# State attention and a hard-swish feed-forward network on one core: the first batch's tokens in two halves with even and odd tokens side by side, half steps for four tiles, and last output tiles scaled whole

## The chip, the core and the metric

The kernel runs on one core of a Trainium2 chip. The core has TensorE (PE) for matmuls, VectorE (DVE), ScalarE (ACT) and GpSimd (POOL), and SyncE (SP), whose queue issues most transfers. The metric is the device time of one execution in microseconds, the median of the runs shown.

## The reference

The input `x` has 8 batches of 8 heads, 512 tokens and 64 columns, and `state` has 32 state tokens for each batch and head. Tokens attend to states, and states to tokens; both results go through one network.

```python
scores = scale * x @ state.T ; a  = softmax(scores) ; xread = a @ state       # 512 tokens of a head
scores2 = scale * state @ x.T; a2 = softmax(scores2); sread = a2 @ x          # 32 states of a head
x = concatenate([xread, sread], tokens)   # as rows of 512 columns (8 heads x 64): 8 x 544 rows
h = x @ w_in                              # w_in 512 x 2048
g = h * clip(h + 3, 0, 6) / 6
out = g @ w_out                           # w_out 2048 x 512, out 4352 x 512 in float32
```

The weights lie in DRAM as 64-bit floats, and the kernel makes 32-bit values of them.

## The kernel before

**Steps.** The network is done in 144 steps of 128 of its 2048 inner columns: 16 steps for the 512 tokens of each batch, and 16 for the state reads of all batches together (b = 8). A step has a first product into a PSUM bank `ps_h` (`first`), ScalarE and VectorE make `g` of it, and a second product adds into four banks `acc` (`second`). Since `a @ state @ w_in` is the same as `a @ (state @ w_in)`, the kernel makes W' = state x W_in for each batch and chunk of four steps (`wprime`, L441) and multiplies the attention weights by it, so that the token reads themselves are never made. Nearly all products are sums of three products of rounded high and low parts (`product`, L733). The first four steps of batch 0 are plain float32 (L762 and L800). Steps run in segments: batch 0's first four, batch 1's first four, the rest of batch 0, more of batch 1, then the batches one by one, and the states' steps last.

**Weights.** `weight` loads a tile of W_in or W_out (L303), and turns 64-bit into 32-bit words: ScalarE takes low digits and scales (L308, L312), VectorE clamps, joins and sets the sign (L316, L320, L327). The first tiles are unpacked while the first batch's attention runs.

**Batch 0.** Its x is loaded into a staging tile by two transfers of four heads each, and VectorE copies it into `xb` (L414). A partition p holds the four neighbouring tokens 4p to 4p+3. TensorE turns the state (L489) and x (L510, into banks that ScalarE copies to `xT`, L515), makes scores by rows of tokens in two halves (L565), each of which needs all four parts of `xT`, and VectorE and ScalarE do a softmax along the 32 states (L527 maximum, L529 subtraction, L531 exponential, L533 sum, L537 multiplication). The result is turned back (L582) and copied to `a` (L587). The first step's product needs `a` of all 512 tokens. The states' own attention uses the scores by columns (`scores_by_columns`: four heads' 32 states as 32-column groups, 512 tokens wide, L441 in `all_heads`), exponentials, eight transposes (L663) and a read (L678). Batch 1 takes its scores by columns as well.

**Order.** The class `Plan` collects each instruction group with an engine (`T` TensorE, `V` VectorE, `S_` ScalarE, `Q` a transfer of SP), a cost and a rank, and a list scheduler sets the order of each engine from them when the program is built. Where it leaves TensorE nothing to do before the first step, fillers are put in (transposes of the identity into `ps_h`, L1026). Their number is fixed in the program.

**End.** The 256 rows of state reads are two output tiles of 128 x 512. Each is scaled by 1/6 in two column halves, one on ScalarE and one on VectorE (L824), and each half is stored by a transfer of its own (L857 on SP's queue, L854 on ScalarE's).

## Time and profile before

| | |
|---|---|
| median of 3 runs | 676.68 us (676.36 to 677.1) |
| profiled execution | 676.72 us, of which the span is 674.7 us |
| TensorE busy | 666.1 us (99%) |
| VectorE, ScalarE busy | 412.8 us (61%), 317.8 us (47%) |
| packets of transfers | 94429, 41.53 MB |

The span is the part between the first and the last event that the profiler shows; some 2.0 us lie outside it. Times in the trace count from the span's start. Busy shares are means over the whole span; the start, with its short dependent pieces of work, is another matter than the long row of matmuls behind it.

### The profile page before, as it was taken

To read this page: it belongs to the slowest core of one execution; us is meant where nothing else is said; L and a number is where in the kernel's file an instruction comes from. 1 tells how busy PE (TensorE), PEld (TensorE's weight loads), DVE (VectorE), ACT (ScalarE), POOL (GpSimd) and SP (SyncE) were. 2 spreads that over 40 slices of the span, in tenths; PEclk is the share of its full clock that TensorE was granted. 3 is DMA by queue.
4 is the path that set the end of the run, shared out by engine and by line. 5 is a ranking of instruction groups with operands and counts; after the bars stand their busy time and mean duration, and the time that the engine had idled before them with its cause. 6 is when DMAs were issued, how large, how long until landed. Compare 5 with 4: busy or idle time off the path is not lost.

```text
span 674.7 us, 9940 instructions
## 1 busy us (share of the span) xinstructions
PE 666.1 (99%) x4039; PEld 508.6 (75%) x4039; DVE 412.8 (61%) x702; ACT 317.8 (47%) x537; POOL 1.0 (0%) x7
## 2 busy tenths in 40 slices
...
GB/s 260 306 4 149 120 204 82 74 69 125 1 140 53 1 63 78 52 1 63 0 129 1 63 1 103 27 44 21 44 20 1 1 1 63 1 1 0 63 1 31
DMA packets 94429, 41.53 MB, mean 62 GB/s; under 512 B 82480, under 2 KB 85040, under 8 KB 94256
## 3 DMA queue, kind: packets, MB, share of 16 engines
...
q10 hardware_dynamic: 144, 0.13, 0.1%
q14 instruction: 14, 0.11, 0.1%
...
## 4 chain that ended last, share of the span: by engine, by line
PE 96%; DVE 1%; DMA 1%; ACT 1%; issue 0%; SPq 0%
PE acc L733 55%; PE ps_h L733 29%; PE ps_s L441 6%; PE acc L800 2%; PE ps_s L678 1%; PE ps_h L762 1%; PE ps_s L663 1%; DMA st_raw<-in_state_dram 1%; PE acc L510 0%; DVE early L320 0%; DVE s L533 0%; DVE tmp L537 0%; PE acc L582 0%; PE ps_s L693 0%; ACT tmp L531 0%
## 5 line engine op out<-in xcount | busy, mean ns | idle before, releaser
L733 PE MATMUL acc<-w_out_hi,g_hi 128*128 128x512 f32 x528 | 212.1, 402 | 0.0
L733 PE MATMUL acc<-w_out_hi,g_lo 128*128 128x512 f32 x528 | 206.2, 391 | 0.0
L733 PE MATMUL acc<-w_out_lo,g_hi 128*128 128x512 f32 x528 | 205.7, 390 | 0.0
L781 ACT ACTIVATE g<-ps_h,three 128x512 f32<-128x512 f32 (+1 forms) x144 | 95.6, 664 | 214.2 <-PE ps_h L733 212.5
L783 DVE SCALAR_TENSOR_TENSOR g<-g,ps_h 128x512 f32<-128x512 f32 (+1 forms) x144 | 94.1, 654 | 161.2 <-ACT g L781 161.2
L733 PEld LDWEIGHTS acc<-w_out_hi,g_hi 128*128 128x128 f32 x528 | 99.3, 188 | 47.6 <-ACT g L781 21.0
L246 ACT CAST g_hi<-g 128x512 fp32r<-128x512 f32 (+1 forms) x140 | 83.4, 597 | 86.0 <-DVE g L783 86.0
L247 DVE TENSOR_TENSOR g_lo<-g,g_hi 128x512 fp32r<-128x512 f32 (+1 forms) x140 | 91.6, 655 | 47.7 <-ACT g_hi L246 46.6
L733 PE MATMUL ps_h<-aT_hi,wp_hi 128*128 128x512 f32 (+1 forms) x312 | 116.3, 373 | 0.0
L733 PEld LDWEIGHTS acc<-w_out_hi,g_lo 128*128 128x128 f32 x528 | 99.1, 188 | 21.7
L733 PE MATMUL ps_h<-aT_hi,wp_lo 128*128 128x512 f32 (+1 forms) x312 | 114.6, 367 | 0.0
L733 PE MATMUL ps_h<-aT_lo,wp_hi 128*128 128x512 f32 (+1 forms) x312 | 114.6, 367 | 0.0
L733 PEld LDWEIGHTS acc<-w_out_lo,g_hi 128*128 128x128 f32 x528 | 99.3, 188 | 18.5
L733 PEld LDWEIGHTS ps_h<-aT_hi,wp_hi 128*128 128x128 f32 x312 | 58.8, 188 | 13.0 <-issue 2.2
L733 PEld LDWEIGHTS ps_h<-aT_lo,wp_hi 128*128 128x128 f32 x312 | 58.8, 188 | 10.8 <-issue 0.5
L733 PEld LDWEIGHTS ps_h<-aT_hi,wp_lo 128*128 128x128 f32 x312 | 58.8, 188 | 9.8
L247 DVE TENSOR_TENSOR wp_lo<-ps_s,wp_hi 128x512 fp32r<-128x512 f32 (+1 forms) x68 | 42.0, 637 | 3.8 <-ACT wp_hi L246 3.8
L246 ACT CAST wp_hi<-ps_s 128x512 fp32r<-128x512 f32 (+1 forms) x68 | 36.2, 549 | 7.5 <-PE ps_s L441 7.4
L441 PE MATMUL ps_s<-w_in,stT 64*32 64x512 f32 (+1 forms) x592 | 37.3, 561 | 0.0
L441 PEld LDWEIGHTS ps_s<-w_in,stT 64*32 64x32 f32 x592 | 6.7, 104 | 14.3 <-issue 10.9
L308 ACT ACTIVATE early<-early,eighth 128x1024 uint32<-128x1024 uint32 (+1 forms) x14 | 16.1, 1150 | 2.3 <-DMA early<-in_moe_w_in_dram 2.3
L531 ACT ACTIVATE tmp<-tmp 128x512 f32<-128x512 f32 x16 | 10.1, 631 | 14.5 <-DVE tmp L529 14.4
(103 smaller groups left out, 434.3 us busy)
## 6 DMA issues: line engine op xcount, KB each, us to landing
...
raw<-in_moe_w_out_dram SPq DMA_DIRECT2D x7, 512.0 KB, 7.7
ot<-in_x_dram SPq DMA_DIRECT2D x2, 512.0 KB, 3.4
early<-in_moe_w_in_dram SPq DMA_DIRECT2D x2, 512.0 KB
```

The lines of the kernel that those rows point to most:

```text
L246: S_(cost, rank, lambda: nc.scalar.copy(hi(), src()), reads, [writes[0]])
L247: V(cost, rank, lambda: nc.vector.tensor_tensor(lo(), src(), hi().bitcast(F32), op=ALU.subtract), [*reads, writes[0]], [writes[1]])
L308: nc.scalar.activation(low, low, AF.Identity, scale=0.92 * 2.0**-29, bias=eighth)
L441: nc.tensor.matmul(out[u][cols, :], made["stT", b][rows, cols], moving(q)[rows], start=True, stop=True,)
L531: S_(0.62, rank(2), lambda: nc.scalar.activation(bt(), bt(), AF.Exp, scale=SCALE), [], [bt_key])
L663: nc.tensor.transpose(bank(pe[g])[:, js], tmp(e_key[g])[:, js], ident)
L678: nc.tensor.matmul(bank(pr)[cols, u * D : (u + 1) * D], tmp(t_key[u])[:, j * P + q * NS : j * P + (q + 1) * NS], x_tile(b)[:, NG * q + u, ...
L733: nc.tensor.matmul(ps, l, r, start=start and k == 0, stop=stop and k == n - 1)
L762: nc.tensor.matmul(bank(ps), made["wp_32", (b, k)][:, g, fs], a_first(g), start=g == 0, stop=g == NG - 1)
L781: S_(cost + 0.05, n, lambda: nc.scalar.activation(g(), bank(ps)[:, :width], AF.Relu, bias=three), [ps], [g_key])
L783: V(cost, n, lambda: nc.vector.scalar_tensor_tensor(g(), g(), 6.0, bank(ps)[:, :width], op0=ALU.min, op1=ALU.mult), [ps], [g_key])
L800: nc.tensor.matmul(bank(acc), made["g_hi", n][:, js], plain_out[i][1](), start=opens, stop=closes)
```

## The change

The change has these parts.

- **x of batches 0 and 1 in another order.** A partition holds tokens of two halves k of 256 tokens, and of each half an even and an odd token i side by side, so that one transpose turns one head's 2 x 64 columns. Batch 0's x comes by two transfers, one for each half, straight into `xb`, without the staging tile and the copies. Batch 1's comes by one transfer. VectorE makes half of batch 0's copies to `xT`.
- **The state turned twice.** Since even and odd tokens now lie on the two halves of the partitions, the state is needed on both: four matmuls with the identity in place of one transpose.
- **Scores by halves.** The scores by rows of one half need only `xT` of that half. Scores by columns of batches 0 and 1 are 32 matmuls of 128 columns in place of 8 of 512, and the states' softmax takes its maxima and sums over two banks.
- **Half steps.** Each of the first four steps is done as two half steps of 256 tokens: two first products of 256 columns, a gate for each, and two second products for each. W' of these steps comes in four parts and is kept beside `a`, in the place of the third chunk of W_in.
- **Other ranks.** The ranks of the early loads, unpackings, scores and of the states' attention are other numbers, tiles 2 and 3 of W_in are loaded one by one, and what makes high and low parts of the first four W_out tiles is set earlier.
- **The end.** The two last tiles are scaled whole, the first by VectorE, the second by ScalarE, and stored by one transfer each, the first on SP's queue, the second on ScalarE's.

```diff
+        if b >= TURNED:
             for j in range(J):
                 def load(j=j):
-                    nc.sync.dma_start(x_tile(b)[:, :, j, :], x_v[b, j])
+                    nc.sync.dma_start(x_all(b)[:, j], x_v[b, j])
                 Q(rank, 262.144, load, writes=[(*key, j)], after=after)
...
+        elif b == 1:
+            Q(rank, 1048.576, lambda: nc.sync.dma_start(
+                x_all(1).rearrange("p k h i d -> p h k i d"),
+                x[1].rearrange("h (p k i) d -> p h k i d", k=2, i=2)), writes=[(*key, 0)], after=after)
+        else:
+            for k in range(2):
+                def load(k=k):
+                    nc.sync.dma_start(
+                        x_all(0)[:, k], x[0].rearrange("h (k p i) d -> k p h i d", k=2, i=2)[k])
+                Q(rank[k], 524.288, load, writes=[(*key, k)], after=after)
...
         st = ("ps_s", ("st", b))
+        if b < TURNED:
+            def turn_states():
+
+                for i in range(2):
+                    for u in range(NG):
+                        nc.tensor.matmul(bank(st)[i * D : (i + 1) * D, u * P : (u + 1) * P],
+                                         made["st_raw", b][:, u, :], ident, start=True, stop=True)
+
+            def put_state():
+                stT = get(("stT", b), lambda: att.tile([P, NG, P], F32, name="stT"))
+                nc.vector.tensor_copy(stT, bank(st)[:, : NG * P].rearrange("p (u n) -> p u n", u=NG))
+        else:
...
+            rank_q = rank if b else rank(q // 2)
+            T(0.45, rank_q, turn, [x_keys(b)[q // 2 if b == 0 else 0]], [ps], after)
+            if b == 0 and q % 2:
+                V(0.66, URGENT, lambda q=q, ps=ps: nc.vector.tensor_copy(xT(b, q), bank(ps)), [ps], [xT_key(b, q)])
+            else:
+                S_(0.6, rank_q, lambda q=q, ps=ps: nc.scalar.copy(xT(b, q), bank(ps)), [ps], [xT_key(b, q)])
...
         def scores(k):
-            out = bank(ps[k]).rearrange("p (j u q n) -> p j q u n", j=J // 2, u=NG, n=NS)
-            for j in range(J // 2):
-                for q in range(NQ):
-                    js = slice((k * J // 2 + j) * P, (k * J // 2 + j + 1) * P)
-                    nc.tensor.matmul(
-                        out[:, j, q], xT(b, q)[:, js], apart[:, q],
-                        start=True, stop=True,
-                    )
+            out = bank(ps[k]).rearrange("p (i u q n) -> p q u i n", i=2, u=NG, n=NS)
+            for head in range(H):
+                nc.tensor.matmul(
+                    out[:, head // NG, head % NG], xT_of(b, head, k), apart[:, head // NG, head % NG],
+                    start=True, stop=True,
+                )
         for k in range(2):
-            scores_at[b] = T(1.85, rank(1), lambda k=k: scores(k),
-                             [("apart", u) for u in range(NG)]
-                             + [xT_key(b, q) for q in range(NQ)], [ps[k]], after(1))
+            scores_at[b] = T(1.85, rank(1, k), lambda k=k: scores(k),
+                             [("apart", i) for i in range(2)]
+                             + [xT_key(b, 2 * k + g) for g in range(2)], [ps[k]])
...
         ps = [("ps_s", (name, b, u)) for u in range(NG)]
-        T(1.37, rank, lambda: all_heads(
+        def by_halves():
+            for u in range(NG):
+                for k in range(2):
+                    for q in range(NQ):
+                        for i in range(2):
+                            cols = slice((2 * u + k) * P, (2 * u + k + 1) * P)
+                            nc.tensor.matmul(
+                                bank(ps[i])[q * NS : (q + 1) * NS, cols], st_of(b, u, q, i),
+                                xT_of(b, NG * q + u, k)[i * D : (i + 1) * D],
+                                start=True, stop=True,
+                            )
+        T(1.37, rank, by_halves if b < TURNED else lambda: all_heads(
             b, [bank(k) for k in ps], lambda q: xT(b, q)),
...
+        def run():
+            for g in range(NG):
+                nc.tensor.matmul(bank(ps)[:, ts], early_32()[:, NG + g, fs], a_first()[:, g, ts],
+                                 start=g == 0, stop=g == NG - 1)
+        at = T(0.97, rank, run,
+               [("w_in2", "a", k)] + [("w_in2", "a", "wp", f0, u) for u in range(NG)], [ps])
+        first_of.setdefault(n, at)
+        g = lambda: get(g_key, lambda: gp.tile([P, S], F32, name="g", tag="g_hi", bufs=3))[:, ts]
+        S_(0.45, rank, lambda: nc.scalar.activation(g(), bank(ps)[:, ts], AF.Relu, bias=three), [ps], [g_key])
+        V(0.42, rank, lambda: nc.vector.scalar_tensor_tensor(
+            g(), g(), 6.0, bank(ps)[:, ts], op0=ALU.min, op1=ALU.mult), [ps], [g_key])
+
+    def second_plain(n, k, rank):
+        _, i, opens, closes = steps[n]
+        for j in range(2 * k, 2 * k + 2):
+            acc = (f"acc{j}", segment_of[n])
+
+            def run(j=j, acc=acc):
+                nc.tensor.matmul(bank(acc), made["g_hi", (n, k)][:, j * P : (j + 1) * P],
+                                 plain_out[i][1](), start=opens, stop=closes)
+            T(0.9, rank, run, [("g_hi", (n, k)), (*plain_out[i][0], "lo")], [acc])
+
...
         for j in range(nt):
             acc = (f"acc{j}", seg)
             rank = n + LAG
-            if b == B:
-
-                for h, add in enumerate((S_, V)):
-                    cols = slice(h * DO // 2, (h + 1) * DO // 2)
-                    mul = nc.scalar.mul if h == 0 else nc.vector.tensor_scalar_mul
-                    add(0.4, rank, lambda j=j, acc=acc, cols=cols, mul=mul: mul(
-                        ot()[:, j, cols], bank(acc)[:, cols], 1.0 / 6.0), [acc], [(*ot_key, j, h)])
-                continue
             if more:
                 V(0.68, rank, lambda j=j, acc=acc: nc.vector.scalar_tensor_tensor(
                     ot()[:, j, :], bank(acc), 1.0 / 6.0, ot()[:, j, :], op0=ALU.mult, op1=ALU.add),
                     [acc], [(*ot_key, j)])
-            elif j % 2 == 0 or i < NF - 1:
+            elif (j % 2 == 0 or i < NF - 1) if b < B else j == nt - 1:
                 S_(0.62, rank, lambda j=j, acc=acc: nc.scalar.mul(ot()[:, j, :], bank(acc), 1.0 / 6.0),
                    [acc], [(*ot_key, j)])
...
-                for h in range(2):
-                    cols = slice(h * DO // 2, (h + 1) * DO // 2)
-                    if h == 0 and j == nt - 1:
-
-                        S_(0.4, n, lambda j=j, rows=rows, cols=cols: nc.scalar.dma_start(
-                            ov[rows, :, cols], ot()[:, j, cols]), [(*ot_key, j, h)])
-                    else:
-                        Q(n, 131.0, lambda j=j, rows=rows, cols=cols: nc.sync.dma_start(
-                            ov[rows, :, cols], ot()[:, j, cols]), [(*ot_key, j, h)])
+                store = lambda queue, j=j, rows=rows: queue.dma_start(ov[rows], ot()[:, j, :])
+                if j < nt - 1:
+                    Q(n, 262.0, lambda store=store: store(nc.sync), [(*ot_key, j)])
+                else:
+
+                    S_(0.6, n, lambda store=store: store(nc.scalar), [(*ot_key, j)])
...
+    LOADS = {"st": -69.59, "x": (-35.98, -14.54)}
     LATE_TOLD = (8, 12)
-    LATE, LATE_STEP, HALVES = (2.0, 6.0), (0.5, 0.5), 1.0
+    LATE, LATE_STEP, HALVES = (-18.25, 9.43), (-0.09, -24.22), 40.72
+    SOFT, HALF, WPRIME, BACK = (-15.08, -56.86), (-19.16, -5.53), (-25.34, -20.68, -23.92, -4.95), ("acc0", "acc3")
...
-                parts = [(0, 1), (1, 2), (2, FPC)]
+                parts = [(0, 1), (1, 2), (2, 3), (3, 4)]
...
-    at(6, lambda: [f(6.6 + 0.2 * k) for k, f in enumerate(late_halves)])
-    at(9, halves_of_first, 9.5)
+    at(6, lambda: [f(5.69 + 0.2 * k) for k, f in enumerate(late_halves)])
+    at(9 if PLAIN == FPC else PLAIN, halves_of_first, 9.5 if PLAIN == FPC else HALVES)
...
-    load_x(0, -9.0)
+    load_state(0, LOADS["st"])
+    load_x(0, LOADS["x"])
...
-    take_in(0, -5.0, (), accs)
-    tokens_by_rows(0, lambda k: -3.0, lambda k: (), accs)
-    load_x(1, -4.5)
+    load_state(1, -67.33)
+    take_in(0, lambda k: (-24.58, 0.11)[k], (), [f"acc{q}" for q in range(NQ)])
+    tokens_by_rows(0, lambda piece, k: SOFT[k], BACK)
+    load_x(1, 35.75)
...
-            take_in(1, 1.0, [scores_at[0]])
-            rank1 = lambda k: (1.0, 1.2, 1.6, 2.0, 2.4)[k]
-            tokens_by_columns(1, rank1, scores_by_columns(1, 1.2, [wp_at[0, 0, 2]]))
+            take_in(1, -41.50, [scores_at[0]])
+            rank1 = lambda k: (5.68, -17.79, -10.35, -22.47, -29.59)[k]
+            tokens_by_columns(1, rank1, scores_by_columns(1, -20.50, [wp_at[0, 0, 2]]))
```

SP's queue began with one half of batch 0's x (by heads), the state, and the other half of x, with the weights behind. It now begins with the state, a tile of W_in, the first half of x (by tokens), a second tile of W_in, a tile of W_out, and the second half of x.

**VectorE from its start to the first softmax.** `m` is the maximum of the first scores. Before:

```order
L414 COPY xb<-ot 128x2x4x64 x2
L495 COPY stT<-ps_s 128x128
L554 COPY sread_t<-stT 64x4x32 x2
L414 COPY xb<-ot 128x2x4x64 x2
L316 TENSOR_SCALAR early_103<-early_103 128x512
L320 SCALAR_TENSOR_TENSOR early_103<-early_103 128x512
L327 SCALAR_TENSOR_TENSOR w_in_206<-early_103 128x4x128
L316 TENSOR_SCALAR early_103<-early_103 128x512
L320 SCALAR_TENSOR_TENSOR early_103<-early_103 128x512
L327 SCALAR_TENSOR_TENSOR w_in_206<-early_103 128x4x128
L527 TENSOR_REDUCE m_227<-ps_s 128x16
L529 TENSOR_TENSOR tmp<-ps_s,m_227 128x512
```

Now:

```order
L508 COPY stT<-ps_s 128x256
L578 COPY sread_t<-stT 64x4x2x32 x2
L317 TENSOR_SCALAR early_100<-early_100 128x512
L321 SCALAR_TENSOR_TENSOR early_100<-early_100 128x512
L538 COPY xT<-acc_156 128x512
L328 SCALAR_TENSOR_TENSOR w_in_167<-early_100 128x4x128
L317 TENSOR_SCALAR early_100<-early_100 128x512
L321 SCALAR_TENSOR_TENSOR early_100<-early_100 128x512
L328 SCALAR_TENSOR_TENSOR w_in_167<-early_100 128x4x128
L552 TENSOR_REDUCE m_221<-ps_s 128x16
L554 TENSOR_TENSOR tmp<-ps_s,m_221 128x512
```

The four copies of x (L414) are gone, a copy to `xT` (L538) has come in, and the order of unpacking and maximum is the same.

**TensorE around the first step.** L489 and now L503 turn a state, L582 and now L605 turn weights of tokens back, L510 and now L532 turn x of batch 1, L1026 and now L1100 are fillers, L762 and now L807 are the first products. L588 are scores by rows, L633 scores by columns. Before:

```order
L489 MATMUL ps_s<-ident,st_raw 128x128
L1026 MATMUL ps_h<-ident 128x128 x7
L582 MATMUL acc_296<-ident,tmp 128x128 x4
L510 MATMUL ps_s<-ident,ot 128x128 x8
L1026 MATMUL ps_h<-ident 128x128 x8
L510 MATMUL ps_s<-ident,ot 128x128 x4
L1026 MATMUL ps_h<-ident 128x128 x5
L582 MATMUL acc_344<-ident,tmp 128x128 x4
L510 MATMUL ps_s<-ident,ot 128x128 x4
L1026 MATMUL ps_h<-ident 128x128 x2
L762 MATMUL ps_h<-w_in_307,wp_220 128x512 x4
L441 MATMUL ps_s<-w_in_206,stT 32x256 x8
```

Now:

```order
L588 MATMUL ps_s<-sread_t,xT 128x2x32 x8
L503 MATMUL ps_s<-ident,st_raw 64x128 x4
L605 MATMUL acc_274<-ident,tmp 128x128 x4
L1100 MATMUL ps_h<-ident 128x128 x5
L633 MATMUL ps_s<-xT,stT 32x128 x32
L807 MATMUL ps_h<-w_in_200 128x256 x2
L605 MATMUL acc_338<-ident,tmp 128x128 x4
L807 MATMUL ps_h<-w_in_200 128x256 x6
L532 MATMUL ps_s<-ident,ot 128x128 x16
L823 MATMUL acc_403<-raw,g 128x512
```

The first products now begin ahead of the second turn back and of all transposes of batch 1's x, and batch 0's scores by columns stand ahead of them.

**VectorE behind the first softmax half.** `nm` and `r` belong to the states' weights, `g` is a gate, `raw` the first tile of W_out. Now:

```order
L671 TENSOR_TENSOR nm_336<-nm_336 128x2
L673 TENSOR_SCALAR nm_336<-nm_336 128x2
L814 SCALAR_TENSOR_TENSOR g<-g,ps_h 128x256
L317 TENSOR_SCALAR early_153<-early_153 128x512
L321 SCALAR_TENSOR_TENSOR early_153<-early_153 128x512
L328 SCALAR_TENSOR_TENSOR early_153<-early_153 128x512
L683 TENSOR_TENSOR r_357<-r_357 128x2
L685 TENSOR_SCALAR r_357<-r_357 128x2
L686 RECIPROCAL r_357<-r_357 128x2
L814 SCALAR_TENSOR_TENSOR g<-g,ps_h 128x256
L321 SCALAR_TENSOR_TENSOR raw<-raw 128x512
L328 SCALAR_TENSOR_TENSOR raw<-raw 128x512
```

Before, that tile's unpacking stood between the softmax halves and right behind them:

```order
L529 TENSOR_TENSOR tmp<-ps_s,m_252 128x512
L316 TENSOR_SCALAR raw<-raw 128x512
L320 SCALAR_TENSOR_TENSOR raw<-raw 128x512
L533 TENSOR_REDUCE s_317<-tmp 128x16
L535 TENSOR_SCALAR s_317<-s_317 128x16
L536 RECIPROCAL s_317<-s_317 128x16
L537 TENSOR_TENSOR tmp<-tmp,s_317 128x512
L327 SCALAR_TENSOR_TENSOR raw<-raw 128x512
```

The unpacking has moved behind the states' maxima and three gates.

## Rows read from the trace of the kernel before

**Rows 1.** Whole span: busy time of each engine, and the ending chain's shares.
```profile
PE 666.1 (99%) x4039; PEld 508.6 (75%) x4039; DVE 412.8 (61%) x702; ACT 317.8 (47%) x537; POOL 1.0 (0%) x7
...
PE 96%; DVE 1%; DMA 1%; ACT 1%; issue 0%; SPq 0%
```
**Rows 2.** Stretches: busy time of each engine, clock, DMA share, GB/s.
```profile
25.20:50.00 24.80, 24.80 (x118) 10.14 (x117) 24.24 (x40) 21.28 (x33) 0.00 (x0) 1.00 0.30 104
```
**Rows 3.** Chain that ended last, first 60 us: start, duration, what.
```profile
2.02 4.22 DMA st_raw<-in_state_dram
```
**Rows 4.** Timeline, TensorE: start, busy time, instructions of one line.
```profile
1.56 3.89 PE L1026 MATMUL ps_h<-ident 128*128 128x128 f32 x17 [1.56 <-POOL ident masks.py:199]
...
6.38 0.45 PE L489 MATMUL ps_s<-ident,st_raw 128*128 128x128 f32 x1 [0.93 <-DMA st_raw<-in_state_dram]
6.62 1.91 PE L510 MATMUL acc<-ident,xb 128*128 128x128 f32 x8
...
11.18 3.68 PE L565 MATMUL ps_s<-sread_t,xT 128*128 128x64 f32 x32
...
16.76 2.19 PE L1026 MATMUL ps_h<-ident 128*128 128x128 f32 x18
...
20.73 1.04 PE L510 MATMUL ps_s<-ident,ot 128*128 128x128 f32 x8
...
25.25 3.67 PE L762 MATMUL ps_h<-w_in,wp 128*128 128x512 f32 x8
```
**Rows 5.** Timeline to 20 us, VectorE and ScalarE.
```profile
7.75 0.76 DVE L414 COPY xb<-ot 128x512 f32<-128x512 f32 x2
...
11.21 0.76 ACT L308 ACTIVATE early<-early,eighth 128x512 uint32<-128x512 uint32 x1
...
16.15 0.68 DVE L527 TENSOR_REDUCE m<-ps_s 128x16 f32<-128x512 f32 x1
...
19.50 0.68 DVE L537 TENSOR_TENSOR tmp<-tmp,s 128x512 f32<-128x512 f32 x1
```
**Rows 6.** Issue of the first state load, and the page's row on x loads.
```profile
1.25 1.33 SPq L375 DMA_DIRECT2D st_raw<-in_state_dram  x2
...
ot<-in_x_dram SPq DMA_DIRECT2D x2, 512.0 KB, 3.4
```
**Rows 7.** Timeline: one tile's W', a join, scores by columns, a state read.
```profile
14.80 0.45 PE L441 MATMUL acc<-w_in,stT 64*32 64x128 f32 x16
...
28.63 0.69 DVE L320 SCALAR_TENSOR_TENSOR raw<-raw 128x512 uint32<-128x512 uint32 x1
...
37.40 1.09 PE L441 MATMUL ps_s<-xT,stT 64*32 64x512 f32 x16
...
70.48 1.10 PE L678 MATMUL ps_s<-xb,tmp 128*32 128x64 f32 x64
```
**Rows 8.** Packets and rate, 5 to 8 us and 14 to 15 us.
```profile
DMA packets 1030, 0.96 MB, mean 320 GB/s; under 512 B 112, under 2 KB 1030, under 8 KB 1030
...
DMA packets 910, 0.23 MB, mean 233 GB/s; under 512 B 909, under 2 KB 909, under 8 KB 910
```
**Rows 9.** Timeline from 668 us: the last matmul, scaling and stores.
```profile
669.11 0.42 DVE L824 TENSOR_SCALAR ot<-acc 128x256 f32<-128x256 f32 x1 [1.54 <-PE acc L733]
...
669.37 0.39 PE L733 MATMUL acc<-w_out_hi,g_lo 128*128 128x512 f32 x1
669.57 0.38 ACT L824 ACTIVATE ot<-acc 128x256 f32<-128x256 f32 x1 [2.46 <-DVE ot L824]
...
669.98 1.96 SPq L857 DMA_DIRECT2D out_dram<-ot  x3
...
670.66 0.66 ACTq L854 DMA_DIRECT2D out_dram<-ot  x1
```
**Rows 10.** Whole scalings by ScalarE and VectorE: ns minimum, median, maximum.
```profile
L832 ACT ACTIVATE ot<-acc x20: 587/600/632, 51.3 to 627.3; 128x512 f32<-128x512 f32 x20
...
L835 DVE TENSOR_SCALAR ot<-acc x12: 682/692/692, 262.1 to 627.6; 128x512 f32<-128x512 f32 x12
```

255 lines of the change are left out of this document (134 added, 121 removed).

## Prediction

> **What bounds the kernel now.** I began with the page's totals. TensorE is busy in 99% of the span, and the chain that ended last is 96% TensorE [rows 1]. So three things set the time: when the first feed-forward tile starts, how much TensorE does and waits after that, and what follows the last matmul. The start of the timeline gives the first: the first tile runs at 25.25 us [rows 4], and from there TensorE has work up to 669.76 us [rows 9]. The table of stretches says who is scarce just after the first tile: from 25.2 to 50 us VectorE is busy for 24.24 of 24.80 us, ScalarE for 21.28 [rows 2]. VectorE works in program order, so whatever is put into that stretch delays what stands behind it.
>
> Ahead of the first tile the chain starts with the state's transfer, which lands at 2.02 + 4.22 = 6.24 us [rows 3]. Transposes, scores and a softmax follow. The timeline shows where that sequence is stretched: VectorE takes the maximum of the first scores only at 16.15 us, although those scores end by 13.1 us (16 of 32 records of 115 ns from 11.18) [rows 4, 5]. It is held by the unpacking of two tiles of W_in, which ScalarE begins at 11.21 us, after four copies of turned x. From the maximum the softmax is a fixed chain, 16.15 to 19.50 + 0.68 = 20.18 us; the second half follows 3.9 us later, and the first tile needs both.
>
> TensorE runs slowly at first. The clock column reads 1.00 throughout, but a filler takes 3.89/17 = 229 ns at 1.56 us and 2.19/18 = 122 ns at 16.76 us, and eight transposes take 1.91 against 1.04 us: twice the price, the lower of the two levels (1.2 and 2.4 GHz) [rows 4]. The records shorten at about 10.4 us, after TensorE had worked without a pause since 6.4 us.
>
> **The new start.** I took every engine's new order, gave each instruction the duration of the nearest row, and let it start when its engine is free and its inputs are there.
>
> The state is now first in SP's queue. It was second, issued from 1.25 us on [rows 6], and landed 4.22 us after the first of its two issues. With its issue half a microsecond earlier and no x in front of it, I put its landing at 3.7 us: half of the 4.22 us went by while the 512 KB of x ahead of it were moved. The wider memset on POOL delays the identity to about 1.9 us; nine fillers end at 3.9. The state's turn is now four float32 matmuls, which stand in the trace as two records each: 8 x 0.2 = 1.6 us at the lower level, to 5.5 us. Ten fillers (2.2 us) reach 7.7, by when the first half of x is there: its transfer is the third issue, and a 512-KB transfer of before landed 3.4 us after its issue [rows 6]. Eight transposes end at 8.7 to 9.5, ScalarE and VectorE copy one half each (0.6 and 0.7 us). VectorE, without the copies of x out of its staging tile (0.76 us for two [rows 5]), joins the first W_in tile between those, W' follows at 10.1, and eight score matmuls of one half (16 of the 115-ns records, 1.84 us) end at 12.5. The maximum starts at 12.6 in place of 16.15: 3.6 us earlier, because the first half's scores need only half of x, and the two unpackings ahead of the maximum, which ScalarE now begins at 5.5 in place of 11.21, are done by 12.1.
>
> The chain of that half, at the old durations but with a clamp and a copy of xT in it, ends at 16.9. The turn back stands behind the turn of batch 1's state (0.9 us) and ends at 18.4. ScalarE's copy to `a` stands behind the second half's exponential and ends at 19.7; meanwhile TensorE does batch 0's scores by columns (18.9 to 20.15), which stood behind the first tiles before. So the first half tile starts at 20.2 us: 25.25 - 20.2 = **5.05 us earlier**. It needs one half of the tokens; the other half's chain, ending at 21.1, no longer holds it.
>
> **What is given back in work.** Behind the new start, TensorE does more. The sixteen transposes of batch 1's x (at 20.73 and after: 1.04/8 = 0.13 us of record, 0.108 us of pace each) moved behind it, 1.72; the second turn back, 0.43; W' in one more part, 0.24; sixteen half products in place of eight, 0.24. Batch 0's scores by columns went ahead of it, -1.1. Two calls of the new form remain, each 1.2 where the old one took 1.09 [rows 7], +0.2. Sum **+1.7 us**.
>
> The new scores by columns, 32 matmuls of 128 columns for 8 of 512, are not in the trace of before. Two rows are near: W' of one tile, 16 records of just this shape in 0.45 us, 28 ns each with the run-out of the last one in it, and the state read, 64 records of 64 columns in 1.10 us, 17 ns each [rows 7]. With the run-out (about 0.2 us) counted once, the first row paces at 16 to 17 ns too, so 64 x 16 + 0.2 = 1.2 us. The bounds are 1.1 (no more than the old form) and 1.8 (64 x 28 ns). I take 1.2, on which the two rows agree. The Trainium skill's page "TensorE: Matmul & The Clock Gate", section "Wait — 56ns, not 53.3ns?", says that starts of matmuls never come closer than about 25 ns, however small they are; by it the form would take 64 x 25 = 1.6 us, 0.4 us more in each of three calls, an estimate. The row at 17 ns goes below that floor, so I keep the row.
>
> **What is given back in waits.** In the trace of before TensorE shows no wait from 25.2 to 50 us: busy 24.80 of 24.80 [rows 2]. The same walk through the old order gives 1.4 us of waits after the first tile, so that much is the method's own error. In the new order it gives 4.0 us, nearly all before 50 us:
> - The first product with W_out has to wait until VectorE has joined that tile. Ahead of it stand the whole second softmax half (from 17.15), the maxima for the state weights, three half gates and another tile's unpacking: at 0.69 us for a join [rows 7] it is done at 27.6, where TensorE is free at 27.0: 0.64.
> - Batch 1's transposes wait for their PSUM banks to be copied out by ScalarE: 0.63.
> - The state read waits for ScalarE's second copy: 0.56.
> - Two second halves of tile 2 wait for VectorE's gate, which stands behind batch 1's softmax: 0.26 and 0.81.
> - The rest (half tiles, the turn back, the later batches) is 1.1.
>
> Less the 1.4 that the trace does not bear out, that is **+2.6 us**. Bounds: 1.5, if the waits at ScalarE's copies are such an error as well, and 4.0, if nothing of it is; there is no cover, since VectorE had 0.56 us to spare in 24.8 [rows 2].
>
> Startup in all: -5.05 + 1.7 + 2.6 = **-0.75 us**.
>
> **Transfers.** x of batch 0 and 1 is now loaded in packets of 512 bytes and 1 KB; no row has them alone. Stretches with packets of mostly 1 KB moved 320 GB/s, those of 256 bytes 233 [rows 8]. Two 512-KB loads at either rate take 1.6 or 2.25 us each; in the walk the first has 0.5 us of slack under fillers, the second more. The sum takes nothing for it.
>
> **The tail.** Before, the two last tiles were scaled in halves, and ScalarE's halves waited for VectorE's on the same bank (its row at 669.57 names VectorE). Three stores were issued by SP from 669.98 in 1.96 us, to 671.94, and the span ends at 674.7 [rows 9]. Now VectorE scales tile 0 whole: 669.11 + 0.69 = 669.80, SP issues one store of about 0.65 us. ScalarE scales tile 1 whole when the last matmul is done: 669.8 + 0.60 = 670.45, and its queue issues the other by 671.14 [rows 9, 10]. The last issue ends 0.8 us earlier. Each store moves 256 KB in place of 128, and 128 KB at 320 GB/s [rows 8] are 0.4 us, if the last store's end waits for all of them. The whole amount is the same in both kernels and starts earlier now, so I stay nearer to the issues: **-0.7 us** (bounds -0.4 and -0.8).
>
> **Sum.** 676.72 (the profiled execution; the median of the runs is 676.68) - 0.75 - 0.7 = 675.27, so **675.2 us**. A measurement of this kernel can tell about 0.2%, 1.35 us, from no change: what is below 675.3 counts as faster, so my value lies on that line.
>
> **Rivals.**
> - *The startup's gain is eaten whole.* VectorE is the bound from 17 to 50 us. If the small matmuls cost 1.8 (0.6 more in each of three calls) or nothing of the 4.0 us of waits is error, startup comes out at +0.6 to +1.05 us and the tail alone remains: 676.6 to 677.1. For it speaks VectorE's 98% in that stretch; against it that its instructions there get no longer, and that the state read shows small matmuls at 17 ns.
> [...]
> - *More is kept.* If the waits grow by 1.5 us only, and the clock rises by 7 us, so that the first tile starts at 19.9: 675.27 - 1.1 - 0.3 = 673.9.
>
> **Chances.** My forecast 0.62, with its own range from 674.3 to 676.3 (the price of the small matmuls down to 1.1 and waits of 2.0; or either of them 0.9 us more). Its middle is just under the line, so 0.37 of it is faster and 0.25 within 0.2%. Gain eaten: 0.20, all within. Slower: 0.10. More kept: 0.08, faster. So faster 0.45, same 0.45, slower 0.10. The range 673.9 to 676.9 leaves out the slower rival and the upper end of the first.
>
> **What would show it.** In the trace of after: state landing near 3.7 us, VectorE's first maximum near 12.6, the first half tile near 20.2, scores by columns about 1.2 us for 64 records, the first product with W_out near 27.6 waiting for VectorE, about 4 us of waits of TensorE by 50 us, the last matmul some 0.75 us earlier, and the last issue of a store ending about 1.4 us after the last matmul. I am wrong if the low level lasts beyond 10.5 us, if the small matmuls take over 1.5 us, or if VectorE falls further behind between 25 and 50 us.

## The result and the profile after

The changed kernel takes 676.82 us (median of 22 runs, 676.3 to 679.03), the kernel before on the same chip 676.2: ratio 1.0013, 95% interval 1.0007 to 1.0019. That is slower by 0.6 us between the medians and by about 0.9 us by the ratio, less than the 0.2% that counts as a difference here. One execution of the kernel before took 2335.82 us and stays out of the ratio. The first profile of the changed kernel is of one of its longer executions (678.66 us, of which more below). A second one, of the run `a_again` below, is of 676.93 us, near the median; "after" is that second profile unless the text says otherwise. In it L823 are the products with W_out that belong to the first products, and L814 is the gate on VectorE.

First after's TensorE in the timeline: start, busy time, what, and in brackets the idle time before it and who ended it.

```profile
3.88 1.22 PE L503 MATMUL ps_s<-ident,st_raw 128*64 128x128 f32 x8
5.03 2.13 PE L1100 MATMUL ps_h<-ident 128*128 128x128 f32 x10
8.04 1.09 PE L532 MATMUL acc<-ident,xb 128*128 128x128 f32 x8 [0.88 <-DMA xb<-in_x_dram]
...
10.90 2.00 PE L588 MATMUL ps_s<-sread_t,xT 128*128 128x64 f32 x16
...
19.20 1.32 PE L633 MATMUL ps_s<-xT,stT 64*32 64x128 f32 x64
20.45 1.13 PE L807 MATMUL ps_h<-w_in 128*128 128x256 f32 x4
...
26.52 1.14 PE L532 MATMUL ps_s<-ident,ot 128*128 128x128 f32 x8 [0.24 <-ACT w_in L540]
28.10 1.17 PE L823 MATMUL acc<-raw,g 128*128 128x512 f32 x2 [0.44 <-DVE raw L328]
...
37.03 1.16 PE L633 MATMUL ps_s<-w_in,stT 64*32 64x128 f32 x64
...
41.17 2.07 PE L823 MATMUL acc<-raw,g 128*128 128x512 f32 x4 [0.16 <-DVE g L814]
...
50.23 2.07 PE L823 MATMUL acc<-raw,g 128*128 128x512 f32 x4 [1.50 <-DVE g L814]
```

The turn of the state starts at 3.88, that of the first half of x at 8.04, and VectorE's maximum comes at 12.93 (16.15 before [rows 5]). The first half tile runs at 20.45 in place of 25.25 [rows 4], 4.80 us earlier. Then come the waits that the kernel before did not show, small ones and one of 1.50 us.

The stretch just after the first tile, in after (busy time and instructions of TensorE, weight loads, VectorE, ScalarE, GpSimd; clock; DMA share; GB/s), against [rows 2]:

```profile
25.20:50.00 24.80, 22.69 (x242) 11.99 (x241) 20.74 (x43) 19.97 (x37) 0.00 (x0) 1.00 0.24 77
```

TensorE has lost its full occupation, and yet VectorE is less busy than before (20.74 against 24.24 us), and ScalarE too. Neither is short of time in sum. What holds TensorE is told by after's chain that ended last (start, duration, what):

```profile
35.01 6.48 DMA early<-in_moe_w_in_dram
41.51 1.21 ACT early L309
42.72 0.52 ACT tmp L556
43.27 0.70 DVE s L558
...
45.22 0.72 DVE tmp L651
45.96 0.63 ACT aT_hi L246
46.61 0.69 DVE aT_lo L247
47.30 0.61 DVE s L558
...
49.16 0.71 DVE tmp L651
49.87 0.32 DVE g L814
50.23 3.87 PE acc L823 x8
```

Batch 1's softmax goes back and forth between ScalarE and VectorE, each in its fixed order; the gate of a half tile stands behind it, and TensorE waits for that gate. One link is a load of W_in tiles 6 and 7 that could be issued only at 35.01, when its place was free, and took 6.48 us.

At the end, after's last scalings, the last matmul and the two stores:

```profile
669.61 0.69 DVE L906 TENSOR_SCALAR ot<-acc 128x512 f32<-128x512 f32 x1 [1.54 <-PE acc L792]
...
669.86 0.39 PE L792 MATMUL acc<-w_out_hi,g_lo 128*128 128x512 f32 x1
670.29 0.60 ACT L903 ACTIVATE ot<-acc 128x512 f32<-128x512 f32 x1 [2.67 <-PE acc L792]
670.33 0.65 SPq L925 DMA_DIRECT2D out_dram<-ot  x1
670.91 0.66 ACTq L925 DMA_DIRECT2D out_dram<-ot  x1
```

The last issue ends at 671.57, 1.32 us after the last matmul (1.4 forecast; 2.18 before, 671.94 against 669.76 [rows 9]). But the execution ends 6.68 us after the last matmul, against 6.97 before.

The accounts, each from its own execution. "Work" is TensorE's busy time from the first tile to the end of the last matmul, "waits" its idle time there: in after the four that the timeline names (2.34 us) and 0.15 us in smaller gaps. The third column is the kernel before with the new end alone (an experiment below).

| us | before | after | new end alone |
|---|---|---|---|
| first tile | 25.25 | 20.45 | 24.48 |
| work | 644.50 | 647.31 | 644.40 |
| waits | 0 | 2.49 | 0 |
| behind the last matmul | 6.97 | 6.68 | 6.57 |
| time of the execution | 676.72 | 676.93 | 675.45 |

So 4.80 us are gained at the start, 2.81 given back as work and 2.49 as waits, 0.29 gained at the end. The last column shows also how much the start varies from one execution to another: 24.48 and 25.25 with the same start. Two more profiles with the old start have their first tile at 24.32 and 25.40 (`twice_before` and `before_noclamp` below), so the 25.25 is on the late side.

### The profile page after: what moved, and what is told of

Its sections match the earlier page's. It is cut to its first block, busy times and chain, and to the rows that moved or that the text cites. A ratio compares the mean times of both kernels' runs of the same rounds, so it can differ in the third digit from the quotient of the medians.

```text
span 676.8 us, 10273 instructions
## 1 busy us (share of the span) xinstructions
PE 665.1 (98%) x4199; PEld 510.1 (75%) x4199; DVE 415.4 (61%) x708; ACT 319.6 (47%) x548; POOL 1.2 (0%) x7
## 3 DMA queue, kind: packets, MB, share of 16 engines
q1 hardware_dynamic: 92128, 40.64, 22.5%
## 4 chain that ended last, share of the span: by engine, by line
PE 94%; DVE 2%; DMA 2%; ACT 1%; issue 0%; SPq 0%
PE acc L792 55%; PE ps_h L792 28%; PE ps_s L448 6%; PE ps_s L737 1%; PE acc L823 1%; PE ps_s L721 1%; DMA early<-in_moe_w_in_dram 1%; DMA xb<-in_x_dram 1%; PE ps_s L588 1%; DVE tmp L562 0%; DVE s L558 0%; PE acc L532 0%; ACT tmp L556 0%; PE ps_h L1100 0%; DVE tmp L651 0%
## 5 line engine op out<-in xcount | busy, mean ns | idle before, releaser
L792 PE MATMUL acc<-w_out_hi,g_hi 128*128 128x512 f32 x528 | 212.0, 401 | 0.0
L792 PE MATMUL acc<-w_out_hi,g_lo 128*128 128x512 f32 x528 | 206.3, 391 | 0.0
L792 PE MATMUL acc<-w_out_lo,g_hi 128*128 128x512 f32 x528 | 205.7, 390 | 0.0
L864 ACT ACTIVATE g<-ps_h,three 128x512 f32<-128x512 f32 (+1 forms) x140 | 93.1, 665 | 213.9 <-PE ps_h L792 213.9
L866 DVE SCALAR_TENSOR_TENSOR g<-g,ps_h 128x512 f32<-128x512 f32 (+1 forms) x140 | 91.4, 653 | 158.9 <-ACT g L864 158.9
L792 PEld LDWEIGHTS acc<-w_out_hi,g_hi 128*128 128x128 f32 x528 | 99.2, 188 | 47.5 <-ACT g L864 20.9
L792 PEld LDWEIGHTS acc<-w_out_hi,g_lo 128*128 128x128 f32 x528 | 99.1, 188 | 21.9
L792 PE MATMUL ps_h<-aT_hi,wp_hi 128*128 128x512 f32 (+1 forms) x312 | 115.3, 369 | 0.0
L792 PE MATMUL ps_h<-aT_hi,wp_lo 128*128 128x512 f32 (+1 forms) x312 | 114.6, 367 | 0.0
L792 PE MATMUL ps_h<-aT_lo,wp_hi 128*128 128x512 f32 (+1 forms) x312 | 114.6, 367 | 0.0
L792 PEld LDWEIGHTS acc<-w_out_lo,g_hi 128*128 128x128 f32 x528 | 99.3, 188 | 18.6
L792 PEld LDWEIGHTS ps_h<-aT_hi,wp_hi 128*128 128x128 f32 x312 | 58.8, 188 | 11.8 <-issue 1.1
L792 PEld LDWEIGHTS ps_h<-aT_lo,wp_hi 128*128 128x128 f32 x312 | 58.8, 188 | 10.5 <-issue 0.3
L792 PEld LDWEIGHTS ps_h<-aT_hi,wp_lo 128*128 128x128 f32 x312 | 58.8, 188 | 9.8
L246 ACT CAST wp_hi<-ps_s 128x512 fp32r<-128x512 f32 (+1 forms) x68 | 36.3, 549 | 10.4 <-PE ps_s L448 10.4
L448 PE MATMUL ps_s<-w_in,stT 64*32 64x512 f32 (+2 forms) x576 | 35.4, 548 | 0.0
```

Source lines behind the costliest of these rows:

```text
L246: S_(cost, rank, lambda: nc.scalar.copy(hi(), src()), reads, [writes[0]])
L448: nc.tensor.matmul(out[u][cols, :], st_of(b, u, q, u), moving(q)[rows], start=True, stop=True,)
L792: nc.tensor.matmul(ps, l, r, start=start and k == 0, stop=stop and k == n - 1)
L864: S_(cost + 0.05, n, lambda: nc.scalar.activation(g(), bank(ps)[:, :width], AF.Relu, bias=three), [ps], [g_key])
L866: V(cost, n, lambda: nc.vector.scalar_tensor_tensor(g(), g(), 6.0, bank(ps)[:, :width], op0=ALU.min, op1=ALU.mult), [ps], [g_key])
```

## Experiments

The theories in the expectations: **A**, x lands late, TensorE pauses, its clock falls, and the first half tile slips; **B**, the late W_in tile holds ScalarE and so the chain; **C**, at the end the moving of 512 KB from the first issue on sets the time; **D**, the 1.5-us wait is a matter of where one gate stands on VectorE; **V**, VectorE's supply (its work and order together) is what TensorE waits for; **W**, late transfers or ScalarE are. In edits called MOVED, an operation of the finished plan is taken out and put ahead of another; the numbers count the operations in the order in which the code adds them. All ratios are to the kernel before, on the same chip, with their 95% interval.

**The changed kernel again, and the new end alone.** The second is the kernel before with this part of the diff only:

```diff
-            elif j % 2 == 0 or i < NF - 1:
+            elif (j % 2 == 0 or i < NF - 1) if b < B else j == nt - 1:
...
+                store = lambda queue, j=j, rows=rows: queue.dma_start(ov[rows], ot()[:, j, :])
```

> The changed kernel as it is, for a second profile: its first profile is 678.8 us, 2 us above the median of its runs, so something in it varies. Theory A (the first half of x and the W_in tile ahead of it land late, so TensorE pauses 2.3 us, falls to the lower level, and the first half tile starts at 22.1 in place of 20.2): the landing at 8.5 us comes again within 0.5 us, since the queue's order causes it, and the first half tile starts at 21 to 22.5. Theory B (a W_in tile that lands at 43.2 us holds ScalarE, and VectorE and TensorE behind it): the 1.6-us wait of TensorE at 51.9 us comes again in most executions. If neither comes again, the first profile was an outlier and the usual loss of 0.6 to 0.9 us lies elsewhere. Time: 676.8, ratio to before 1.0013.

> The kernel before with the new end alone: two whole scalings and two stores in place of four halves and four stores. My forecast says 0.7 us faster. The trace of the changed kernel says otherwise: its last matmul ends 4.8 us before the span's end, against 4.94 before, and the packets of both kernels move for 2.1 us from about 1.2 us after the first store's issue. So theory C (the moving of 512 KB sets the end, from the first issue on): 0.1 to 0.2 us faster, too little to tell, and packets that end 2.0 us after the last issue in place of 1.5.

Again: 677.09 us, 1.0008 (0.9999 to 1.0017). New end alone: 676.18, 0.9993 (0.9983 to 1.0003). So the end brings 0.4 us in its profile (6.57 against 6.97); in the runs the interval includes no change as well as the 0.7 us of the forecast. The new start, with what it brings behind it, costs about 0.9 us between the two medians. The loss lies there. Of the changed kernel's first profile the late x did not come again (8.04 in place of 8.59, the first half tile at 20.45 in place of 22.08, where A expected 21 to 22.5), but B's long wait did (1.50 us).

**x ahead of the first W_in tile** in SP's queue (after, else the same):

```diff
+    MOVED = [(1, 27)]
```

> The changed kernel with one move in SP's queue: the first half of x ahead of the first W_in tile. No engine's order is changed. Theory A: x lands about 1.2 us earlier (7.0 to 7.5 us), TensorE's pause before its transposes shrinks to under 1.2 us, the maximum of the first scores comes earlier than 14.56, unless the W_in tile (needed by W' ahead of the scores on TensorE) now lands as much later; the two share the transfer engines, so I expect between 0 and 0.9 us of gain. Theory B: no change of the wait at 51.9 us.

680.57 us, 1.0056 (1.0044 to 1.0069). TensorE in its timeline, and its stretch from 10.4 to 25.2 us:

```profile
6.54 1.09 PE L537 MATMUL acc<-ident,xb 128*128 128x128 f32 x8
7.47 1.26 PE L1105 MATMUL ps_h<-ident 128*128 128x128 f32 x10
11.82 0.45 PE L453 MATMUL acc<-w_in,stT 64*32 64x128 f32 x16 [3.10 <-DVE w_in L333]
12.21 3.67 PE L593 MATMUL ps_s<-sread_t,xT 128*128 128x64 f32 x16
...
24.20 1.13 PE L812 MATMUL ps_h<-w_in 128*128 128x256 f32 x4
```
```profile
10.40:25.20 14.80, 13.38 (x164) 11.50 (x164) 10.50 (x21) 8.75 (x18) 0.00 (x0) 0.77 1.07 367
```

x is there 1.5 us sooner, but now W_in is late: TensorE pauses 3.10 us for W', the granted clock falls to a mean of 0.77 in this stretch, and the same 16 records of scores take 3.67 us in place of 2.00. The first half tile comes 3.75 us later than in after, where a gain of 0 to 0.9 us was expected. Much the same happens in the changed kernel itself, in its first profile (678.66 us). Its timeline of TensorE, and behind it its stretches up to 25.2 us:

```profile
8.59 1.97 PE L532 MATMUL acc<-ident,xb 128*128 128x128 f32 x8 [2.33 <-DMA xb<-in_x_dram]
...
22.08 1.13 PE L807 MATMUL ps_h<-w_in 128*128 128x256 f32 x4
```
```profile
0.00:10.40 10.40, 6.30 (x36) 5.53 (x37) 2.21 (x7) 3.43 (x6) 1.17 (x7) 0.89 0.73 221
10.40:25.20 14.80, 14.46 (x186) 11.94 (x185) 12.57 (x25) 10.54 (x21) 0.00 (x0) 0.96 1.07 364
```

There the ten fillers ran out early (1.31 us in the timeline, where after's took 2.13 at the lower level), x came half a microsecond later, TensorE paused 2.33 us, and eight transposes took 1.97 us where after's take 1.09. So A's mechanism is real and worth 1.6 us in that execution, but after's median is reached without it.

What comes behind the first half tile is hardly touched by this. From there to the end of the last matmul x_first takes 649.69 us and after's first profile 649.91, against 649.80 in after and 644.51 before. The 5.3 us are given back whether the first half tile runs at 20.45, 22.08 or 24.20.

**Six more fillers** ahead of x's transposes, so that no pause remains:

```diff
                             idle()
+                    if n == 42:
+                        for _ in range(6):
+                            idle()
```

> The changed kernel with sixteen in place of ten fillers ahead of the transposes of x, so that TensorE has no pause of 0.9 to 2.3 us there. Theory A as it now stands (a late x lets TensorE pause, and in some executions it falls back to the lower level for its transposes, as in the first profile): executions above 677.6 go away, the low end stays, and the median falls by 0 to 0.3. If at the lower level the sixteen fillers end behind x's landing, they cost up to 0.5 us instead.

677.24 us, 1.0023 (1.0015 to 1.0032). Executions above 677.6 us were to go away; four of eleven are there still. The profile is of one of these (679.12): a load of the state came late in it (a pause of 1.06 us at 4.6 us), the sixteen fillers last, at the lower level, until 10.05 us, and the first half tile runs at 22.41. So nothing is gained; what the fillers cost in an execution near the median is not shown.

**ScalarE's part of W_in tiles 6 and 7 later**, behind batch 1's first exponential:

```diff
+    MOVED = [(169, 197), (170, 197)]
```

> The changed kernel with two of ScalarE's instructions (low digits and scale of the W_in tile that landed at 43.2 us) moved behind the exponential of batch 1's first softmax half and a gate that stood behind them; VectorE takes up this tile only later, so nothing else is held. Theory B: the 1.6-us wait at 51.9 us shrinks by 0.7 to 1.0, and so does the time (ratio to before 1.0000 to 1.0003). Theory A alone: the waits behind are made up elsewhere, no change.

678.57 us, 1.0024 (1.0014 to 1.0035). Four of its nine runs lie at 677.42 to 677.45, the others at 678.57 to 678.94. The profile (677.43 us) is of one of the four, and what lengthens the others is not shown. In it VectorE waits:

```profile
47.09 0.69 DVE L252 TENSOR_TENSOR aT_lo<-tmp,aT_hi 128x512 fp32r<-128x512 f32 x1 [1.25 <-ACT aT_hi L251]
```

The exponential is no longer held: it starts 21.31 us after the first half tile, in after 22.18. But now the two instructions (1.21 and 1.11 us on ScalarE) stand ahead of the next link, the rounding of `aT`, and VectorE waits 1.25 us for that. TensorE's wait at 49 us is 1.78 us. B falls as a story of one late load: in both of the places tried, the chain pays for that work.

**Two gates earlier on VectorE**, then the same with the places of two tiles exchanged:

```diff
+    MOVED = [(147, 121), (157, 127)]
```
```diff
-        ("in", 4): ("early0", 1), ("in", 6): ("early1", 1), ("out", 4): ("early2", 1),
+        ("in", 4): ("early0", 1), ("in", 6): ("early2", 1), ("out", 4): ("early1", 1),
```

> The changed kernel with two gates of VectorE (the second halves of the third and fourth tile) moved ahead of the second softmax half of batch 1, in which they stood: the first ahead of its subtraction, the other ahead of the turn at its end. Theory D (TensorE's 1.5-us wait near 49 us is one for VectorE's order: ScalarE's part of that gate was done 5 us before): the wait shrinks to under 0.3 us, the chain of batch 1 is 0.4 to 0.8 us later, and the time falls by 0.8 to 1.3 us, to 675.6 to 676.1. Theory B (the late W_in tile on ScalarE): with ScalarE still held, the wait goes to the first products of batch 1 and the time falls by at most 0.4.

> As gate_early, and the W_in tile that landed at 41.5 to 43.9 us takes the place of a W_out tile needed later, which frees its load to be issued at 13 us; the plan moves some instructions behind the first eight steps with it. Theory B in its second form (this load costs 0.8 us of VectorE's chain): the exponential of batch 1's first half starts at 41.4 in place of 42.6, and the time is 0.3 to 0.8 us below gate_early. Theory D alone: the same as gate_early.

676.57 us, 1.0003 (0.9994 to 1.0012), and 677.19, 1.002 (1.0011 to 1.0029). With the gates earlier the wait near 49 us is gone, and this one stands in the timeline instead:

```profile
56.83 0.67 PE L453 MATMUL ps_s<-w_in,stT 64*32 64x256 f32 x16 [1.17 <-DVE w_in L333]
```

W' waits for VectorE to join W_in tiles 4 and 5, which is the next thing in VectorE's order. With the places exchanged, waits of 0.88 us at 84 us and 0.33 at 119 us come in its stead. D is right about the place and wrong about the price (675.6 to 676.1 was expected): what one order gives, the next link takes, all but 0.2 us from the first half tile to the last matmul (649.59 against 649.80), and the intervals of the ratios overlap with after's.

**The clamp left out** (VectorE's L317, on all weight tiles but the first two of W_in; the limit on their values is not applied), in after, in before and in gate_early, and in gate_early moved to GpSimd:

```diff
-        V(0.1 + 0.27 * n, rank, clamp, [], [hi])
+        V(0.1 + 0.27 * n, rank, clamp if kind == "in" and k < 2 else lambda: None, [], [hi])
```
```diff
-            nc.vector.tensor_scalar(s, s, LARGEST, -LARGEST, op0=ALU.min, op1=ALU.max)
+            (nc.vector if kind == "in" and k < 2 else nc.gpsimd).tensor_scalar(s, s, LARGEST, -LARGEST, op0=ALU.min, op1=ALU.max)
```

> The changed kernel without the clamp of 64-bit weights on VectorE (it limits weights beyond float32's range) for all tiles but the first two of W_in: some 12 instructions of 0.42 or 0.69 us less on VectorE, about 2.5 us of them before 55 us. Theory V (VectorE's work in its order is what TensorE waits for from 25 to 100 us, so an earlier first tile only turns into waits): TensorE's 2.5 us of waits shrink by 1 to 2 us, and the time falls by 0.8 to 2 us. Theory W (the waits come from late transfers and ScalarE, and VectorE is not short): the wait at 49 us stays at 1.2 or more, and the time falls by less than 0.5.

> The kernel before with the same clamps left out. TensorE has no wait after its first tile there. Theory V: no gain behind the first tile; one clamp (0.42 us) stood in the second softmax half ahead of the first tile, so the time falls by 0 to 0.5 us. If it falls by a microsecond or more, VectorE held the kernel before as well, where the profile shows no wait.

> Both: the changed kernel with the two gates moved ahead (gate_early) and without those clamps. Theory V: with the gates out of the way what is left is VectorE's amount of work, so this falls by 1 to 2 us below gate_early (676.57), to 674.6 to 675.6. Theory W: as gate_early within 0.5.

> The changed kernel with the two gates moved ahead, and the same clamps done by GpSimd, which is idle: all of the computation is kept. Theory V: as gate_noclamp, if GpSimd needs no more than 2 us for a clamp and VectorE's own instructions keep their length, so 674.8 to 676; this would be faster than both kernels. If GpSimd's work lengthens VectorE's instructions beside it, or a clamp takes more than 3 us, the gain is gone.

| | us | ratio | TensorE's waits, us |
|---|---|---|---|
| after without clamp | 676.84 | 1.0011 (1.0002 to 1.002) | 2.48 |
| before without clamp | 676.53 | 1.0009 (1.0 to 1.0018) | 0 |
| gates early, without clamp | 675.98 | 0.9999 (0.9989 to 1.0008) | 1.40 |
| gates early, clamp on GpSimd | 678.34 | 1.0037 (1.0024 to 1.005) | 2.68 |

Less work on VectorE alone changes nothing, which is W's answer: with the clamps gone, the same wait stands at 48.5 us, 1.72 long, at the end of the same chain. With the gates early it does help in the profile, where the stretch from the first half tile to the last matmul is 648.88 us against 649.59 with the clamps; the intervals of the two ratios overlap, and V had asked for 1 to 2 us. The chain then runs through ScalarE without a gap from 50.88 to 56.10 us (six of its seven pieces there):

```profile
50.88 0.62 ACT aT_hi L251
51.51 0.97 ACT wp_hi L251 x2
52.48 1.02 ACT early L318
53.50 0.51 ACT aT_hi L251
54.01 0.98 ACT ot L908 x2
54.99 0.51 ACT aT_hi L251
```

On GpSimd the clamps are slower (the group of lines of that run: busy us, mean ns, idle us before them):

```profile
L322 POOL TENSOR_SCALAR early<-early 128x1024 f32<-128x1024 f32 (+1 forms) x13 | 14.6, 1123 | 80.3 <-ACT early L318 74.2 <-DVE nm L673 6.2
```

The ten of 128x1024 among them take 1.22 us on the mean, where VectorE's in after take 0.69; the chain grew longer, with 1.30 us of wait at 56.5. So neither theory holds as it was put: what TensorE waits for is work and order together (V), on a chain that runs through both engines (W's half).

**More work for TensorE alone.** The rest of the question was whether TensorE's added work counts at all. W' for batch 1's first chunk stands just ahead of the 1.5-us wait; it is multiplied twice or four times into the same banks, in after, in before (162 there) and in gate_early:

```diff
                 self.ops[n][3]()
+                if n == 174:
+                    for _ in range(1):
+                        self.ops[n][3]()
```

> The changed kernel, with the projection of W_in (W') for batch 1's first chunk multiplied twice into the same banks, at 47.6 us, just ahead of TensorE's 1.5-us wait for VectorE's gate near 49 us: 1.0 us more of TensorE's work (16 records of 64x512), no work more for any other engine. Theory V (VectorE's supply is what TensorE's first tile and its work are measured against here): the wait shrinks from 1.5 to about 0.5 us and the last matmul ends where it did: 676.5 to 677.1. Rival (TensorE's own amount of work sets the end, the waits being a part of its chain that comes anyway): 1.0 more, 677.6 to 678.1.

> The changed kernel, with the same W' multiplied four times: 3.0 us more of TensorE's work. Theory V: the first 1.5 us of it replace the wait, the rest shows: +1.5, about 678.4, with no wait near 49 us. Rival: +3.0, about 679.9.

> The kernel before, with the same W' (at 36.6 us there) multiplied twice: a control where TensorE never waits after its first tile. Both theories: 1.0 us more, 677.0 to 677.4. If it were nothing, the doubled product would be hidden in some other way, and the run named twice would tell nothing.

> The changed kernel with the gates of the second halves of tiles 3 and 4 earlier on VectorE (as in gate_early), where the wait near 49 us is gone and one of 1.17 us stands at 55.7 us for the sign of a W_in tile, and W' twice as in the run named twice. Theory V: the 1.0 us is taken out of the wait at 55.7 (about 0.2 left), time as gate_early's, 676.3 to 676.9. Rival (waits are only a matter of TensorE's order, and work adds up): 1.0 more, 677.4 to 677.8.

TensorE in the timelines of "twice" and "four":

```profile
47.77 1.95 PE L451 MATMUL ps_s<-w_in,stT 64*32 64x512 f32 x32
50.52 2.07 PE L826 MATMUL acc<-raw,g 128*128 128x512 f32 x4 [0.80 <-DVE g L817]
```
```profile
47.65 3.66 PE L451 MATMUL ps_s<-w_in,stT 64*32 64x512 f32 x64
51.24 2.07 PE L826 MATMUL acc<-raw,g 128*128 128x512 f32 x4
```

| | us | ratio | work, us | waits, us | first tile to last matmul, us |
|---|---|---|---|---|---|
| after | 677.09 | 1.0008 (0.9999 to 1.0017) | 647.31 | 2.49 | 649.80 |
| twice | 677.12 | 1.002 (1.0011 to 1.0029) | 648.11 | 1.81 | 649.92 |
| four | 678.11 | 1.004 (1.0027 to 1.0052) | 649.75 | 1.00 | 650.75 |
| before, twice | 676.4 | 1.0015 (1.0004 to 1.0025) | 645.13 | 0 | 645.13 |
| gates early | 676.57 | 1.0003 (0.9994 to 1.0012) | 647.43 | 2.16 | 649.59 |
| gates early, twice | 676.66 | 1.0015 (1.0006 to 1.0024) | 648.24 | 1.19 | 649.42 |

A repeat costs 1.95 - 1.09 = 0.86 us. In after it comes out of the wait: 0.80 more work, 0.68 less wait, 0.12 us more to the last matmul. Four other profiles with after's order behind the first half tile unchanged (after's first, x_first, fill16, tail_split) lie at 649.69 to 650.05, so 0.86 more would be seen. Three repeats are 2.57 us; the first 1.50 replace the wait, and the product starts 1.01 us later than in after (51.24 against 50.23). With the gates early the repeat comes out of the wait at 56 us (1.17 becomes 0.20). Before, where nothing waits, the work grows by 0.63 us (1.0 was expected), and the runs are 0.15% longer. Three profiles of three give V's answer: TensorE has room ahead of that gate. The medians differ from those of after, twice and gate_early by 0.03, 0.99 and 0.09 us, which agrees. The ratios do not tell the theories apart: this group's runs of before were 0.4 us faster than the earlier group's, and by them the repeat costs 0.12% in after and 0.15% before, with intervals that overlap.

**The first of the two last tiles in halves** (VectorE one, ScalarE the other, two stores by SP, the last tile whole):

```diff
+            elif b == B and j == 0:
+                for h, add in enumerate((V, S_)):
+                    cols = slice(h * DO // 2, (h + 1) * DO // 2)
...
+                    for h in range(2):
+                        cols = slice(h * DO // 2, (h + 1) * DO // 2)
```

> The changed kernel with its first last tile scaled in two halves (VectorE, then ScalarE) and stored by two transfers; the second tile stays whole on ScalarE. The first store is issued 0.3 us earlier, the last one as before. Theory C (the moving of 512 KB sets the end, from the first issue on): the span ends 0.2 to 0.4 us earlier after the last matmul, time 0 to 0.4 below the changed kernel. The forecast's step (the last issue sets the end): no change.

677.05 us, 1.0011 (1.0003 to 1.002). The first store was issued 0.18 us before the end of the last matmul, where after's was issued 0.08 behind it, and the rest still took 6.74 us (6.68). C in its form "from the first issue on" is not borne out. What the packets show is narrower. GB/s from 669 to 676 us in 40 slices of 0.175 us, before, and then after:

```profile
GB/s 0 0 0 0 0 0 0 0 0 0 0 0 0 158 181 316 106 146 217 334 328 304 345 322 223 18 0 0 0 0 0 0 0 0 0 0 0 0 0 0
```
```profile
GB/s 0 0 0 0 0 0 0 0 0 0 0 0 0 0 0 246 152 152 199 328 386 410 316 316 351 129 12 0 0 0 0 0 0 0 0 0 0 0 0 0
```

Both move 0.52 MB in about 2.1 us, beginning 1.3 us after the first issue. Before, the last packets (673.4) come 1.5 us after the last issue ends, after, 2.0 us after it (673.6 against 671.57). Most of what the issues gain is used up by moving.

## Why the prediction was wrong

My range, 673.9 to 676.9, holds the time, at its upper end, but I forecast 1.5 us less and the runs show 0.6 us more. By steps, against the second profile:

| term, us | forecast | measured |
|---|---|---|
| first tile | -5.05 | -4.80 |
| work behind it | +1.7 | +2.81 |
| waits behind it | +2.6 | +2.49 |
| end | -0.7 | -0.29 |
| sum | -1.45 | +0.21 |

**The start came nearly as forecast.** The turn of the state starts at 3.88 (landing forecast at 3.7), the maximum at 12.93 (12.6), the first half tile at 20.45 (20.2). Only x came later than I put it: its transfer took 5.35 us from the issue, where I had taken 3.4, so the turn of x starts at 8.04 in place of 7.7.

```profile
2.64 5.35 DMA xb<-in_x_dram
```

But the 25.25 from which I counted is on the late side. By the accounts above, a run of before with the median of 676.2 has its first tile at about 676.2 - 6.97 - 644.5 = 24.7, and one of after with 676.82 at about 20.3, an estimate. That makes the gain 4.4 us in the runs, and 0.6 us of loss in all.

**The step that failed is "What is given back in work": I put it at +1.7, and it is +2.81.** I gave each group the price of its row in the trace of before, and nothing more to groups that only change places. The groups of lines show what that left out, first of before from 25.2 to 62 us, then of after from 20.4 to 62 us (busy us, mean ns, idle us before them):

```profile
L800 PE MATMUL acc<-raw,g 128*128 128x512 f32 x24 | 11.7, 620 | 0.0
L762 PE MATMUL ps_h<-w_in,wp 128*128 128x512 f32 x16 | 7.6, 610 | 0.0
```
```profile
L823 PE MATMUL acc<-raw,g 128*128 128x512 f32 x24 | 12.7, 634 | 2.1 <-DVE g L814 1.7 <-DVE raw L328 0.4
L807 PE MATMUL ps_h<-w_in 128*128 128x256 f32 x32 | 8.5, 394 | 0.1
L532 PE MATMUL ps_s<-ident,ot 128*128 128x128 f32 x16 | 2.2, 281 | 0.2 <-ACT w_in L540 0.2
```

The same 24 records of products with W_out are busy for 1.0 us more (forecast nothing), the half tiles for 0.9 more (forecast 0.24), the sixteen transposes for 2.2 (forecast 1.72). That is 2.1 us more than I had counted. The split products give back some 0.9 of it: the 32 records of L792 take 408 ns on the mean, the 36 of L733 before took 436. The products with W_out and the half tiles start anew more often in after, in smaller groups. Which part is the start and the run-out of a group, which is waiting in small pieces and which is the halves' own price, no run separates; that cause stays open.

**The waits came out as forecast, +2.49 for +2.6, in part by luck.** The traces bear out that I took the 1.4 us off: the walk gave 1.4 us for the kernel before, where the trace shows none, and 4.0 for after, where it shows 2.49, so it is too high by 1.4 and by 1.5. Without that, the sum would have been 675.27 + 1.4 = 676.67, near the measured time, but with waits that the trace does not show. In the same way the rival "the startup's gain is eaten whole" came near, with +0.6 forecast and -4.80 + 5.30 = +0.50 measured. Neither of its two conditions came: the small matmuls cost 1.2, and the trace shows 2.49 us of waits, not 4.0. Only if the 1.1 us of added work were waiting in small pieces would its second condition hold in part.

**Where the waits stand was half right.** The first product with W_out waits 0.44 us from 27.66 (0.64 from 27.0), batch 1's transposes 0.24 (0.63), the state read not at all (0.56), two gates 0.16 and 1.50 (0.26 and 0.81). Nearly all of them are shorter than I put them, and the last one is longer. What made that one long I had not seen: ScalarE sits idle for 0.85 us until W_in tiles 6 and 7 are there, and does their low digits ahead of batch 1's exponential. Moving that work (in6_later) brought the exponential 0.87 us forward and did not help: it then held the next link.

**The reason was half right.** I wrote that VectorE, busy 98% of the stretch, is the bound. It is not its sum: after, VectorE is idle for 24.80 - 20.74 = 4.06 us of that stretch, and taking the clamps out gave nothing. It is the sequence of VectorE and ScalarE through batch 1's softmax up to a gate. "Twice" and "four" show that TensorE's work ahead of that gate is free up to 1.5 us: the gate at 49.87 sets the time there. It does not stand still, though, when the start moves. In after's first profile, fill16 and x_first the first half tile is 1.63, 1.96 and 3.75 us later than in after, and the product behind the gate 1.70, 2.05 and 3.62 later. No run moved the first tile without that chain.

**The end was mis-sized**: -0.7 forecast, -0.29 in after and -0.40 with the new end alone. I followed the issues, which do end 0.86 us sooner, and named the 256 KB per store as the bound of -0.4. With the new end alone that bound is the value, and after's lies beyond it.

**Small matmuls and the clock.** Batch 0's scores by columns take 1.32 us and batch 1's 1.16 for 64 records, so 1.2 was right. The Trainium skill's page "TensorE: Matmul & The Clock Gate", section "Wait — 56ns, not 53.3ns?", with its 25 ns between starts would give 1.6, an estimate; the trace does not bear that out. That the low level lasts beyond 10.5 us, one of my signs of being wrong, did not come in after: its fillers up to 7.2 us stand at that level, the transposes from 8.04 on do not. The clock cost time in x_first (680.57) and in after's first profile, by a pause and the fall behind it.
